# A gated long convolution with a squared-ReLU MLP: the short convolution's inputs laid out by time block and channel group

## The chip, the cores and the metric

The kernel runs on one core of a Trainium2 chip. The metric is device time in microseconds for one execution, median of several. The profile names the engines PE (TensorE, matmuls), PEld (its weight loads), DVE (VectorE), ACT (ScalarE), POOL (GpSimd) and SP (SyncE, which here only issues DMA transfers). SBUF is the on-chip memory with 128 partitions, PSUM the accumulator memory that matmuls write, here used as 8 banks of 512 floats per partition.

## What is computed

Sequence length S = 2048, D = 640 channels, F = 1728, everything float32.

```python
mod = (silu(c) @ w_mod).reshape(6, D)              # sa, ca, ga, sb, cb, gb
h = layernorm(x) * (1 + ca) + sa                   # x = A_q
k_shift[t] = sum(k[t - j] * shift_k[:, j] for j in range(4))
kv = k_shift * v
y = causal_conv(kv, ssm_k) + kv * ssm_D            # per channel, length 2048, by FFT of length 4096
x = x + ga * (h * y)
h = layernorm(x) * (1 + cb) + sb
x = x + gb * (relu(h @ w1 + b1) ** 2 @ w2 + b2)
```

## The kernel before

**Two stages.** The first computes the gated convolution, channel block by channel block (5 blocks b of 128 channels). The second is the MLP, over 8 chunks n of 256 rows and 14 slices f of F. The MLP's matmuls take operands split in a high and a low part (`hring`, `xt`, `w_S...`, `w_W`).

**The convolution as matmuls.** Time is split as t = 64 n + i (n is its upper part, 0 to 31, i its lower part, 0 to 63). Two operands per block have n and a channel sub-index a (0 to 3) on the 128 partitions and (32 channel groups, 64 values of i) along the free dimension: tile `p`, whose half 0 is kv and whose half 1 is ssm_k. `unit_a` transforms over n with the small table in `cst` (128 calls for each operand of a block, 256 instructions: the profile's `ps<-cst,p` of 64x64), ACT copies the result into tiles `a`; `spectra` transforms over i with the table `gb` (`ps<-a,gb`); for block 0 the filter's spectra are made first and kept (`early_h`, tiles `hs`); `front` multiplies the two spectra on DVE and combines on POOL (tiles `wx`); `back` and `unit_y` transform back with the tables `gi` (`ps<-gi,wx`) and `ca`; `prep` and `finish` apply layernorm, gate and residual and store the new x to DRAM (`x_d`). Each fp32 matmul call becomes two matmul instructions in the trace, a transpose one.

**Where kv comes from.** `kv_load` brings k and v in their natural layout, time on partitions, in pieces of 512 times by 128 channels (256 KB, runs of 512 bytes). `kv` turns each piece with four PE transposes (`ps<-ident,KV`) so that channels lie on partitions and time along the free dimension. ACT writes the first tap's product (scale by a per-partition `tap`), DVE adds the three others with SCALAR_TENSOR_TENSOR, each reading the transposed piece shifted by one more column; the three columns at a piece's end go through `ktail` and, from block 1 on, through small POOL products `kover`. Then v is transposed, DVE multiplies (`KV<-ps,KV`), and the product goes to a DRAM buffer `kv_d` [640 channels, 2048 times]. `load_x` reads it back in the layout of tile `p` (runs of 256 bytes). `load_h` brings ssm_k in the same layout (20 pieces, 128 partitions each); `skip` adds ssm_D to its value at time 0 on POOL.

**Tables.** `gb` and `gi` are loaded whole (2 MB each, 4 pieces each).

**Modulation rows.** `mod_sum(j)` loads five pieces of w_mod (`wm`), scales each on ACT by silu(c), and adds them on POOL; `mod_row` sums over partitions with two matmul calls against a tile of ones (`ps<-wm,ones`). The last gate row is made instead by `w_gate` matmuls whose weights are silu(c) broadcast to 128 columns.

**Order.** The program is a graph of steps; `order` places the steps of each engine in a list by priorities from a table `URGE`, and each engine then runs its list in order. Buffers have named slots that are handed on in order (`KACC`, `KN`, `UT` are parts of tile `KV`; `work` parts of `WX`). PSUM: any of 8 banks (`ANY`). SP's transfers are issued in order, and each waits until the fourth one before it has landed (`OUT = 4`, in `sp_issue`, L591):

```python
    def sp_issue(o, i):
        nc.sync.dma_start(o, i)
        queued.append(nc.cur_bb.bb.instructions[-1].name)
        if len(queued) > OUT:
            info = mybir.DependencyInfo(mybir.DependencyClass.Sync, mybir.DependencyReason.DATA)
            tc.add_manual_dep(nc.cur_bb.bb.instructions[-1], queued[-1 - OUT], info, reason="place in time")
```

Nearly all other instructions are issued from one place and carry L402 in the profile, so they are told apart by their tiles.

## Time and profile before

| | us |
|---|---|
| median of 3 runs | 699.93 (695.98 to 700.84) |
| the profiled execution's own time | 702.44 |
| its span, first to last instruction | 700.7 |
| mean granted TensorE clock | 0.978 |
| PE busy in the span | 648.1 |
| DVE, ACT, POOL busy | 389.4, 326.4, 253.8 |
| bytes moved by DMA | 74.45 MB |

Times below are those of the profiled execution, counted from the start of its span; its own time is 1.7 us above its span and 2.5 us above the median. The MLP's first matmul of chunk 0 comes at about 299 us, so the span is 299 us of the first stage and 402 us of the second.

### The profile page before, as it was taken

The page shows a single profiled execution, that of the slowest core. Times are in us where ns is not written, and L with a number is a line of the kernel's source. Part 1 is how long each engine was busy: PE and PEld are TensorE (multiplying, and loading weights), DVE is VectorE, ACT ScalarE, POOL GpSimd, SP SyncE. Part 2 cuts the span into 40 slices and gives each one's busy share as a digit, 9 for nine tenths or more (in the row PEclk, how much of TensorE's full clock was granted, in tenths as well). Part 3 has the DMA queues.
Part 4 walks back from the last instruction along what each step waited for, and adds up shares of the span by engine and source line. Part 5 has one row for each costly group of instructions (what it writes and reads, how often), then busy time and mean ns, then how long its engine had stood idle before and what let it go on. Part 6 is the DMA issues. An engine that isn't in the chain of part 4 may idle for free.

```text
span 700.7 us, 17805 instructions
## 1 busy us (share of the span) xinstructions
PE 648.1 (92%) x7513; PEld 582.6 (83%) x7513; DVE 389.4 (56%) x780; ACT 326.4 (47%) x678; POOL 253.8 (36%) x316
## 2 busy tenths in 40 slices
PE   3867998879988999899999999999999999999996
PEld 3766876758877787599999889999999999999996
DVE  0726866576769555875262464375354463563532
ACT  3643667776867786554332253224233243242220
POOL 1125765676867659643211321004013021030000
PEclk9999999998999999999999999999999999999999
DMA  9989889899885535542020020020020020110011
GB/s 245 244 243 294 251 238 225 211 253 220 194 196 135 145 78 182 157 135 61 1 76 1 0 76 1 1 76 1 1 75 1 5 73 2 36 40 1 0 39 38
DMA packets 108788, 74.45 MB, mean 106 GB/s; under 512 B 48546, under 2 KB 95650, under 8 KB 108708
## 3 DMA queue, kind: packets, MB, share of 16 engines
q1 hardware_dynamic: 101600, 70.24, 37.1%
q10 hardware_dynamic: 7044, 3.07, 2.4%
q8 instruction: 59, 0.97, 0.6%
q14 instruction: 21, 0.17, 0.1%
q0 software_dynamic: 64, 0.01, 0.0%
HBM read 58.88 MB, written 14.42 MB: 105 GB/s over the span
## 4 chain that ended last, share of the span: by engine, by line
PE 84%; DMA 6%; issue 3%; DVE 3%; ACT 2%; POOL 1%; SPq 0%; DVEq 0%; ACTq 0%; POOLq 0%
PE ps L402 84%; DMA p<-in_A_ssm_k_dram 2%; DMA KV<-in_A_k_dram 2%; DMA KV<-in_A_v_dram 1%; DVE KV L402 1%; DMA gb<-in_gb_dram 1%; DMA kv_d<-kacc 1%; ACT a L402 1%; DVE up L402 1%; DVE xt L402 0%; ACT KV L402 0%; POOL xt L402 0%; DVE wx L402 0%; SPq L591 0%; POOL x L402 0%
## 5 line engine op out<-in xcount | busy, mean ns | idle before, releaser
L402 PE MATMUL ps<-xt,w_S 128*128 128x512 f32 (+1 forms) x935 | 177.4, 331 | 3.6 <-POOL xt L402 1.6
L402 PEld LDWEIGHTS ps<-xt,w_S 128*128 128x128 f32 x935 | 142.8, 190 | 18.2 <-POOL xt L402 2.1
L402 PE MATMUL ps<-w_S,hring 128*128 128x320 f32 x648 | 109.0, 310 | 0.0
L402 ACT ACTIVATE mtmp<-ps,b1t 128x256 f32<-128x256 f32 (+1 forms) x112 | 51.5, 473 | 115.8 <-PE ps L402 111.4
L402 PEld LDWEIGHTS ps<-w_S,hring 128*128 128x128 f32 x648 | 99.2, 188 | 2.1
L402 PEld LDWEIGHTS ps<-a,gb 128*64 128x64 f32 x1280 | 74.6, 144 | 14.7 <-issue 5.9
L402 PE MATMUL ps<-a,gb 128*64 128x128 f32 x1280 | 83.5, 286 | 3.2 <-DVE wx L402 2.0
L402 DVE TENSOR_TENSOR mtmp<-ps,mtmp 128x256 f32<-128x256 f32 (+1 forms) x99 | 41.2, 420 | 81.4 <-ACT mtmp L402 80.5
L402 PE MATMUL ps<-cst,p 64*64 64x64 f32 x2560 | 50.0, 229 | 23.3 <-issue 12.2
L402 PEld LDWEIGHTS ps<-cst,p 64*64 64x64 f32 x2560 | 44.6, 142 | 31.1 <-issue 14.2
L402 DVE TENSOR_TENSOR hring<-mtmp,hring 128x256 fp32r<-128x256 f32 x74 | 37.3, 510 | 53.3 <-ACT hring L402 52.8
L402 POOL TENSOR_TENSOR wx<-wx 128x256 f32<-128x256 f32 x80 | 58.5, 750 | 16.5 <-DVE wx L402 12.2
L402 POOL TENSOR_TENSOR x<-x,gb2row 128x640 f32<-128x640 f32 x16 | 25.3, 1593 | 93.3 <-ACT mtmp L402 92.5
L402 ACT ACTIVATE hring<-mtmp 128x256 fp32r<-128x256 f32 x74 | 30.2, 414 | 60.6 <-PE ps L402 48.7
L402 ACT ACTIVATE a<-ps 128x512 f32<-128x512 f32 x80 | 45.5, 625 | 23.8 <-PE ps L402 23.6
L402 PE MATMUL ps<-w_S,w_W 128*128 128x320 f32 x312 | 52.7, 308 | 0.0
L402 DVE TENSOR_TENSOR wx<-ps,wx 128x512 f32<-128x512 f32 x64 | 41.1, 680 | 17.3 <-PE ps L402 15.0
L402 POOL TENSOR_TENSOR x<-mtmp,x 128x640 f32<-128x640 f32 (+1 forms) x9 | 13.0, 1450 | 100.4 <-DVE mtmp L402 100.4
L402 PEld LDWEIGHTS ps<-w_S,w_W 128*128 128x128 f32 x312 | 48.1, 188 | 1.1
L402 POOL TENSOR_TENSOR mtmp<-mtmp 128x256 f32<-128x256 f32 (+1 forms) x21 | 14.5, 690 | 83.8 <-ACT mtmp L402 83.5
L402 PE MATMUL ps<-gi,wx 64*128 64x128 f32 x640 | 41.0, 279 | 3.1 <-issue 2.3
L402 POOL TENSOR_TENSOR xt<-xfs,xt 128x256 fp32r<-128x256 f32 x35 | 28.3, 816 | 42.6 <-ACT xt L402 42.5
(130 smaller groups left out, 1070.1 us busy)
## 6 DMA issues: line engine op xcount, KB each, us to landing
wm<-in_w_mod_dram SPq DMA_DIRECT2D x25, 320.0 KB, 3.9
p<-in_A_ssm_k_dram SPq DMA_DIRECT2D x20, 256.0 KB, 5.9
KV<-in_A_k_dram SPq DMA_DIRECT2D x20, 256.0 KB, 4.4
KV<-in_A_v_dram SPq DMA_DIRECT2D x20, 256.0 KB, 4.5
p<-kv_d SPq DMA_DIRECT2D x20, 256.0 KB, 4.5
q<-in_A_q_dram SPq DMA_DIRECT2D x7, 640.0 KB, 7.2
out_dram<-x SPq DMA_DIRECT2D x14, 320.0 KB, 3.6
w1s<-in_B_w_dram SPq DMA_DIRECT2D x13, 320.0 KB, 3.5
```

Of the source, the lines that this page charges most:

```text
L402: fn(*real, **{k: a.real() if isinstance(a, View) else a for k, a in kw.items()})
```

## The change

The short convolution is made directly in the layout of tile `p`. The 640 channels are split in three groups s of 128, 256 and 256 channels (`BASE`, `WIDE`); a group's partition is 32 a + n, its free dimension is (i, channel within a). k and v come in 10 units u of 1024 elements per partition (two of group 0, four each of groups 1 and 2), each as four DMAs of 32 partitions (131 KB, runs of 128 bytes in group 0 and of 256 bytes in the others). A unit of k carries three more columns in front, the times before its own, copied on ACT from the unit before or, in the first, loaded by eight small DMAs that ACT issues. The taps are columns broadcast over i, so a tap's product is a tensor-tensor multiply. The first product goes to a two-bank PSUM tile, the others to SBUF; in groups 0 and 1 two of the four products are on POOL (`KP`); DVE adds them up in PSUM and multiplies by v into the operand of `unit_a`, tile `px` (names `S0p`, `S1p` in the order). There are no transposes of k and v, and no `kv_d`. ssm_k comes in four DMAs of 32 partitions per block.

Also changed: half of `gb` and of `gi` is loaded, the other half is made by ACT with sign changes (a few columns come from `cst`); the modulation rows j = 0, 1, 2 are made as the last gate row was, by ten matmul calls each with weights silu(c) broadcast (`sg4`, which lies in `XP0p`, and `sg1`), without ACT and POOL; q for the gating comes in pieces by channel group s, 128 or 256 channels wide; steps other than these units may use six PSUM banks; `ssm_D` is loaded straight into place by eight small POOL transfers; `URGE` is a new table.

```diff
-        "gb": gb.reshape(128, 4096).astype(f),
-        "gi": gt.reshape(128, 64, 2, 2, 16).transpose(0, 1, 3, 4, 2).reshape(128, 4096).astype(f),
+        "gb": gb[:, :, 0].reshape(128, 2048).astype(f),
+        "gi": gt[:, :, 0].reshape(128, 2048).astype(f),
...
-    banks = [one(i) for i in range(8)]
+    banks = [one(i) for i in range(8)] + [(("B6", "B7"), lambda s, d, n: shaped(last[: s[0]], s))]
...
-    ANY = (0, 1, 2, 3, 4, 5, 6, 7)
+    ANY = (0, 1, 2, 3, 4, 5)
+    BOTH = (8,)
...
+    BASE, WIDE, MATES = (0, P, 3 * P), (DG, 2 * DG, 2 * DG), ((0,), (1, 2), (3, 4))
+    SB = (0, 1, 1, 2, 2)
...
     def mod_sum(j):
+        ts = [psum(f"mr_{j}_{i}", (P, 320), MR) for i in range(2)]
+        for b in range(NB):
+            t = stg(f"wm_{j}_{b}")
+            sp_dma(t, w_mod[b * P : (b + 1) * P, j * D : (j + 1) * D], 2560)
+            for i in range(2):
+                with g.as_one(0.53):
+                    mm(ts[i], sgb(b), t[:, 320 * i : 320 * i + 320], b == 0, b == NB - 1)
...
     def load_gb(i):
+        sp_dma(gb[:, 0, o], gb_d.rearrange("p (g a f) -> p g a f", g=16, a=2)[:, o], 4096)
+        act.activation(gb[0:64, 1, o], gb[64:128, 0, o], AF.Copy, scale=-1.0)
+        act.activation(gb[64:128, 1, o], gb[0:64, 0, o], AF.Copy)
     def load_gi(i):
+        sp_dma(gi[:, 0, o], gi_d.rearrange("p (g c n) -> p g c n", g=16, c=2)[:, o], 4096)
+        act.activation(gi[:, 1, o, 0], gi[:, 0, o, 1], AF.Copy, scale=-1.0)
+        act.activation(gi[:, 1, o, 1], gi[:, 0, o, 0], AF.Copy)
...
-    def kv_load(b, h):
-    def kv(b, h, kn):
...
-            for j in range(4):
-                turn(tk[:, j * P : (j + 1) * P], kn[:, 0, j], hold=[acc])
-        act.activation(acc[:, c:], tk[:, c:], AF.Copy, scale=tap[:, b, 0:1])
-        for t in (1, 2, 3):
-            dve.scalar_tensor_tensor(o, tk[:, : 512 - t], tap[:, b, t : t + 1], o, op0=ALU.mult, op1=ALU.add)
-        dve.tensor_mul(acc, tv, acc)
-        sp_dma(in_dram(kv_d, to, b * P, b * P + P, 1 << h), acc, 2048)
...
+    def load_kv(s, u):
+        w = WIDE[s]
+        n = 1024 // w
+        kt = KT[s, u] = sbuf(f"k_{s}_{u}", (P, n + 3, w), KS, line="K")
+        if u == 0:
+            pool.memset(kt[:, 0:3], 0.0)
+        else:
+            copy(act, kt[:, 0:3], KT[s, u - 1][:, n : n + 3])
+        for a in (0, 2, 1, 3):
+            cols = slice(BASE[s] + w * a, BASE[s] + w * a + w)
+            if u == 0:
+                act_dma(kt[32 * a + 1 : 32 * a + 17, 0:3], kshift[0:16, 0:3, cols], 4 * w)
+                act_dma(kt[32 * a + 17 : 32 * a + 32, 0:3], kshift[16:31, 0:3, cols], 4 * w)
+            sp_dma(kt[32 * a : 32 * a + 32, 3:], ksrc[:, n * u : n * u + n, cols], 4 * w)
+        vt = VT[s, u] = sbuf(f"v_{s}_{u}", (P, n, w), VS, line="V")
+        for a in (0, 2, 1, 3):
+            sp_dma(vt[32 * a : 32 * a + 32], vsrc[:, n * u : n * u + n, cols], 4 * w)
+
+    def kv(s, u):
+        acc = psum(f"kacc_{s}_{u}", (P, n, w), BOTH)
+        for t in range(4):
+            o = sbuf(f"ktmp_{s}_{u}_{t}", (P, n, w), TMP) if t else acc
+            own = t > 1 and s in KP
+            mul(pool if own else dve, o, kt[:, 3 - t : 3 - t + n], taps[:, t].unsqueeze(1).to_broadcast([P, n, w]), hold=[] if own else [acc])
+            if t:
+                add(dve, acc, acc, o)
+        for b in MATES[s]:
+            c = slice(beta(b), beta(b) + DG)
+            mul(dve, px[b][:, :, n * u : n * u + n].rearrange("p g i -> p i g"), acc[:, :, c], vt[:, :, c])
...
+    def load_h(b):
+        for a in (0, 2, 1, 3):
+            c = BASE[SB[b]] + WIDE[SB[b]] * a + beta(b)
+            sp_dma(t[32 * a : 32 * a + 32], hsrc[:, c : c + DG], 256)
+        pool.tensor_add(t[:, :, 0], t[:, :, 0], dsm[:, b])
...
     URGE = {
-        ("b1", 0): [-1812, -1830],
+        ("b1", 0): [-1209, -1601],
```

In the order below, each row is one instruction or several alike (xN), written as output<-inputs and shape; a number at the end of a name is the buffer's. On SP, before: SP's list around the store and the re-load of block 0's kv (`kacc0` is block 0's product, `p_0` its operand tile, `gi` the table).

```order
L591 DMA p_1_146<-in_A_ssm_k_dram 128x8x64
L591 DMA kv_d_98<-kacc0_231 128x512 x4
L591 DMA KV_87<-in_A_k_dram 128x4x128 x2
L591 DMA gi_379<-in_gi_dram 128x1024
L591 DMA KV_87<-in_A_v_dram 128x4x128
L591 DMA kv_d_98<-KV_87 128x512
L591 DMA p_0_102<-kv_d_98 128x8x64 x2
```

And now, from the tenth row of SP's list, the end of group 0's k and v (32x32x32), the first two of ssm_k's four pieces for block 0 (`S1p`), and group 1's first pieces (32x16x64):

```order
L617 DMA KV_87<-in_A_k_dram 32x32x32
L617 DMA gb_134<-in_gb_dram 128x1024
L617 DMA KV_87<-in_A_v_dram 32x32x32 x3
L617 DMA gi_144<-in_gi_dram 128x1024
L617 DMA KV_87<-in_A_v_dram 32x32x32
L617 DMA S1p_150<-in_A_ssm_k_dram 32x32x64 x2
L617 DMA KV_87<-in_A_k_dram 32x16x64 x4
L617 DMA KV_87<-in_A_v_dram 32x16x64
```

The store and the re-load are gone, and ssm_k's pieces, which were first in the queue, stand behind all of group 0's k and v.

On PE, before: the end of the first transform of ssm_k (`p_102`) and the first transposes of k (`ident,KV`), rows 47 to 53 of its list.

```order
L402 MATMUL ps_90<-cst,p_102 64x64 x2
L402 MATMUL ps_91<-cst,p_102 64x64 x2
L402 MATMUL ps_97<-ident,KV 128x128 x4
L402 MATMUL ps_96<-ident,KV 128x128 x4
L402 MATMUL ps_95<-ident,KV 128x128 x4
L402 MATMUL ps_94<-ident,KV 128x128 x4
L402 MATMUL ps_93<-ident,KV 128x128 x4
```

And now, rows 142 to 151, between the spectra of block 0 (`a_0`): the modulation row's matmuls (`wm` pieces by the broadcast silu(c) in `XP0p`).

```order
L402 MATMUL ps_93<-a_0_342,gb 64x128 x8
L402 MATMUL ps_94<-wm_0_553,XP0p 128x320
L402 MATMUL ps_94<-wm_1_565,XP0p 128x320
L402 MATMUL ps_95<-wm_0_553,XP0p 128x320
L402 MATMUL ps_94<-wm_2_589,XP0p 128x320
L402 MATMUL ps_90<-a_0_186,gb 64x128 x8
L402 MATMUL ps_94<-wm_3_603,XP0p 128x320
L402 MATMUL ps_95<-wm_1_565,XP0p 128x320
L402 MATMUL ps_95<-wm_2_589,XP0p 128x320
L402 MATMUL ps_95<-wm_3_603,XP0p 128x320
```

PE's list now starts with the first transform of block 0's kv (`S0p`, 128 calls) and goes on with that of ssm_k (`S1p`); the 160 transposes of k and v are gone, and 24 more modulation calls stand in the early part.

## The prediction on record

> **What bounds the kernel now.** I read the table of stretches first, cut where it matters for this change: 0 to 34, 0 to 89 and 89 to 299 us, one disturbed stretch, and the MLP. Columns: stretch, length, busy us of PE, PEld, DVE, ACT, POOL, granted clock, DMA share, GB/s.
>
> ```profile
> 0.00:34.00 34.00, 20.66 (x400) 18.27 (x402) 13.26 (x30) 15.82 (x29) 4.81 (x17) 1.00 0.94 244
> 0.00:89.00 89.00, 62.51 (x1517) 55.50 (x1520) 46.38 (x91) 43.10 (x80) 31.71 (x62) 0.96 0.90 257
> 89.00:299.00 210.00, 191.57 (x3457) 155.64 (x3445) 146.26 (x237) 150.41 (x296) 144.71 (x175) 0.96 0.74 185
> 120.00:160.00 40.00, 31.53 (x586) 24.99 (x584) 25.54 (x40) 31.16 (x65) 26.09 (x28) 0.89 0.91 232
> 299.00:701.00 402.00, 393.99 (x2556) 371.44 (x2556) 196.78 (x453) 132.88 (x303) 77.34 (x79) 0.99 0.11 32
> ```
>
> In the MLP PE is busy 394 of 402 us; nothing the change touches works there, so I keep that stretch. In the first 299 us PE works 254.1 us and idles 44.9: 26.5 before 89 us, beside DMA engines that are 90% busy, and 18.4 after. The second view is who PE waits for, first until 89 us, then until 299 (us in total, times, longest).
>
> ```profile
> PE ps L402 <- DMA gb<-in_gb_dram: 9.1, 1, 9.1
> PE ps L402 <- DMA KV<-in_A_k_dram: 7.4, 4, 4.9
> PE ps L402 <- issue: 7.3, 5, 2.4
> ...
> PE ps L402 <- issue: 8.8, 6, 2.3
> PE ps L402 <- DVE KV L402: 3.4, 3, 2.7
> PE ps L402 <- DVE wx L402: 2.0, 1, 2.0
> ```
>
> Early, PE waits for the first data (until 9.1 us) and for k; later for its own instructions ("issue"), and for the short convolution on DVE. So the stage is PE's work plus a start set by DMA, and the change must be priced in three sums: PE's work, when data arrive, and DVE.
>
> **PE's work.** The groups by shape (columns: count, busy us, mean ns):
>
> ```profile
> L402 PE MATMUL ps<-ident,KV 128*128 128x128 f32 x160 | 27.7, 314 | 12.3 <-DMA KV<-in_A_k_dram 7.4 <-DVE KV L402 2.7 <-issue 1.6
> L402 PE MATMUL ps<-cst,p 64*64 64x64 f32 x2560 | 50.0, 229 | 23.3 <-issue 12.2 <-DMA gb<-in_gb_dram 9.1 <-POOL p L402 1.4
> L402 PE MATMUL ps<-wm,ones 128*128 128x320 f32 x12 | 5.2, 532 | 0.0
> L402 PE MATMUL ps<-w_gate 128*128 128x320 f32 x20 | 6.7, 448 | 0.0
> ```
>
> Removed: 160 transposes, 27.7 us, and the six modulation calls (12 instructions), 5.2. Added: 30 calls in the form of the gate's ten, 6.7/10 = 0.67 each, 20.1. Net 27.7 + 5.2 - 20.1 = 12.8 us less work, all of it inside the first 299 us. Everything else on PE keeps its count.
>
> **When data arrive.** The transfers (KB each, median us from issue to landing):
>
> ```profile
> p<-in_A_ssm_k_dram SPq DMA_DIRECT2D x20, 256.0 KB, 5.9
> KV<-in_A_k_dram SPq DMA_DIRECT2D x20, 256.0 KB, 4.4
> p<-kv_d SPq DMA_DIRECT2D x20, 256.0 KB, 4.5
> kv_d<-KV SPq DMA_DIRECT2D x16, 256.0 KB, 3.9
> gb<-in_gb_dram SPq DMA_DIRECT2D x4, 512.0 KB, 4.9
> w2s<-in_B_w_dram SPq DMA_DIRECT2D x2, 160.0 KB, 2.8
> ```
>
> Removed: store and re-load of kv, 20 pieces of 256 KB each way, 10.5 MB, and half of both tables, 2.1 MB. At the 257 GB/s of the first stretch these 12.6 MB are 49 us of transfer time. Against that, k, v and ssm_k (15.7 MB) now come in pieces of 32 partitions, which no row shows. With four in flight, the 160 KB pieces (2.8 us, 64 partitions) would give 4 x 160/2.8 = 229 GB/s, the 256 KB pieces of ssm_k, in runs of 256 bytes as the new ones, 4 x 256/5.9 = 174. I take 190, nearer to the row with the same runs; then the 15.7 MB need 83 us where 257 GB/s would need 61. Net some 27 us less for the DMA engines, in a stage whose later part isn't bound by them.
>
> [...]
>
> The start, by SP's new order. The first PE call needs all of group 0's k and v: 2.1 MB at 190 = 11 us, and before their last piece the taps and the first pieces of both tables, 1.4 MB at 257 = 5.4; with 0.7 us to the first issue, 2 for the last landing and one DVE product (below) PE starts at about 21 us, where it started at 9.1:
>
> ```profile
> 9.13 1.99 PE L402 MATMUL ps<-cst,p 64*64 64x64 f32 x64 [9.13 <-DMA gb<-in_gb_dram]
> ```
>
> It then has 256 instructions at 50.0/2560 = 0.0195, 5 us, and waits for ssm_k of block 0, whose fourth piece has 2.1 MB of 32-partition pieces and 0.5 MB of table ahead of it: 11 + 2 us more, 34 with the POOL addition. Everything on PE is queued behind these two waits, and on ACT the first copies of `a`. So PE idles 29 us in the first 34; before it idled 34 - 20.7 = 13.3.
>
> I then compare equal progress: both lists reach a place where 64 `back` calls and 144 calls of spectra are done, before at 89 us, now at row 300. Up to there the new list has 256 first-transform instructions less (5.0 us), no transposes (76 of them, 76 x 0.173 = 13.1), and 20 modulation calls instead of 2 (+11.7): 62.5 - 5.0 - 13.1 + 11.7 = 56.1 us of work, 51 of it after 34 us. That gives 85, and 87 with one stall of the "issue" kind. Row 300 needs block 1's kv: of group 1 and what SP has between, 4.2 MB at 190 and 6.4 MB at 257, 22 + 25 us after 33, 80 us, and the last unit's sums. So the place is reached at 87 instead of 89: the late start is paid back by transposes that are gone and by waits for k that are gone. I put -2.
>
> From there to the MLP the work is 254.1 - 12.8 - 56.1 = 185.2 us. Of the 18.4 us of idle time the 8.8 of "issue" stay, since the first transform that starves PE of instructions is as long as before; the 3.4 on the convolution and some of the rest, which come in a knot of ACT, DVE and POOL at 120 to 160 us, go with the work taken from ACT. I take 12. 185.2 + 12 = 197, against 210: -13.
>
> **DVE, ACT and POOL.** The rows for the price:
>
> ```profile
> L402 DVE SCALAR_TENSOR_TENSOR KV<-ps,tap,KV 128x511 f32<-128x511 f32 x16 | 12.0, 749 | 3.7 <-ACT ktail L402 1.8 <-ACT KV L402 1.5
> L402 DVE TENSOR_TENSOR KV<-ps,KV 128x512 f32<-128x512 f32 x20 | 13.7, 686 | 7.4 <-PE ps L402 4.4 <-ACT wx L402 1.9
> L402 DVE TENSOR_TENSOR mtmp<-ps,gbrow 128x320 f32<-128x320 f32 x32 | 14.3, 484 | 12.0 <-PE ps L402 11.6
> L402 DVE TENSOR_TENSOR up<-up,row 128x512 f32<-128x512 f32 x8 | 5.5, 691 | 8.2 <-ACT up L402 8.2
> L402 DVE TENSOR_TENSOR up<-up,KV 128x512 f32<-128x512 f32 x8 | 8.3, 1064 | 1.5 <-POOL KV L402 1.5
> L402 DVE TENSOR_TENSOR wx<-ps,hs 128x512 f32<-128x512 f32 x16 | 10.1, 683 | 3.9 <-PE ps L402 3.9
> L402 DVE BATCH_NORM_STATS2 s<-q 128x6 f32<-128x320 f32 x30 | 13.1, 473 | 0.0
> L402 POOL TENSOR_TENSOR KV<-KV,row 128x512 f32<-128x512 f32 x12 | 16.7, 1402 | 5.0 <-DVE KV L402 3.5 <-DVE row L402 1.4
> L402 POOL TENSOR_TENSOR wm<-wm,wm 128x640 f32<-128x640 f32 x20 | 31.0, 1550 | 16.6 <-ACT wm L402 11.1 <-ACT ktail L402 5.4
> L402 POOL TENSOR_SCALAR kover<-ktail,tap,kover 128x1 f32<-128x1 f32 x36 | 14.3, 407 | 1.6
> L402 ACT ACTIVATE wm<-wm,sg 128x640 f32<-128x640 f32 x25 | 20.4, 824 | 1.0 <-DMA wm<-in_w_mod_dram 0.8 <-issue 0.2
> L402 ACT ACTIVATE KV<-ps,tap 128x512 f32<-128x512 f32 x4 | 2.8, 688 | 3.8 <-PE ps L402 3.8
> ```
>
> DVE loses 20 x (3 x 0.749 + 0.686) = 58.7 us. An operation with a PSUM operand costs 0.484 at 320 and 0.686 at 512 columns, so 1.22 at 1024. DVE gains 30 sums, 10 products into PSUM and 2 last products at 1.22 (51.2), 16 half-wide last products at 0.686 (11.0), and 18 products from SBUF to SBUF, which no row shows at this size: twice 0.691 to twice 1.064, 25 to 38 us; I take 27, since POOL helps in only twelve products. Sum 89, 30 more than before, and DVE's load in the stage goes from 192.6 to about 223 of 285 us. That is hidden as long as no unit's product is what PE waits for.
>
> POOL gains 12 products of 2 x 1.402 (34) and loses 12 of the 20 `wm` additions (18.6) and `kover` (14.3): even. ACT loses 20 first products (13.8) and 15 scalings (12.4) and gains eight table halves, four of 512 columns (0.69 each) and four of 1024 (up to twice that), 7, and seven short copies and some 31 more DMA issues; these take ACT's queue 0.36 to 0.64 us each:
>
> ```profile
> 1.28 0.64 ACTq L514 DMA_DIRECT2D cst<-in_cw_dram  x1
> 4.30 0.36 ACTq L521 DMA_DIRECT2D cst<-in_ca_dram  x1
> ```
>
> 11 to 20 us, so ACT is even too. The two banks reserved for the units leave six for the rest; among PE's longest waits above none is for ACT, which frees most banks, so I charge nothing, and 3 us at the upper end.
>
> **The sum.** 702.4 (profiled execution) - 2 - 13 = 687.4; that execution is 2.5 above the median, so against the median it is 684.9. I forecast 686, between the two, and 676 to 697 for this case: the DMA bounds (229 and 174 GB/s instead of 190) are worth -4 and +2 us at the start, those of the idle time after 89 us (6 and 18 for 12) -6 and +6, the PSUM banks +3.
>
> **The rivals.** *DVE comes late (slower).* A product that reads two SBUF tiles took 691 ns in one group and 1064 in another of the same shape, the latter next to POOL's additions on the same tiles. [...] On the traced numbers: up to the last product of block 1, DVE's list holds 18 sums, 12 flat products, the last products, 16 spectra products (0.683) and 15 statistics (0.473), 66 us at the low price and 75 at the high one, from about 9 us on. If DVE is busy 85% of the time there, block 1 is ready at 9 + 75/0.85 = 97 instead of 87, and group 2's 16 flat products on DVE repeat it: +10 and +12, 708. It decides when DVE's idle time up to there exceeds 12 us at the low price, 3 at the high one. For it: DVE was idle 43 of the first 89 us, waiting for data, and much of that may stay. Against: at half load a late unit has room to catch up. *The pieces are slow (slower).* If a 131 KB piece takes nearly as long as a 256 KB one, the rate with four in flight falls to 125 GB/s (at 5.9 us it would be 89). Then the start, ssm_k and group 1 each lose 6, 6 and 12 us: +12 to +23, 698 to 709. Against: the 160 KB rows at 2.8 us. *PE's idle time stays.* The work goes, but PE's idle time after 89 us stays at 18.4 since "issue" and PSUM take its place: -6, and nothing at the start: 694 to 699. *More comes back.* With 229 GB/s the early place is reached 5 us sooner, idle after 89 us falls to 5 (-7 more), and the clock, 0.89 in the disturbed stretch (3.5 us of its 31.5), comes back: 686 - 5 - 7 - 4 = 670, down to 667. That the change does not do what it says is excluded by the order: no transposes, no `kv_d`.
>
> **Chances.** Forecast 0.45, more 0.16, idle stays 0.10, DVE late 0.17, slow pieces 0.12. A change of 1%, 7 us, is about what a measurement of this kernel can tell from none. Under 693: 0.40 of the forecast, all of "more", 0.01 of the third: 0.57. Over 707: most of DVE late (0.13) and of the slow pieces (0.09): 0.22. Between: 0.21. Range 667 to 711: it leaves out the worse halves of the two slow cases.
>
> **What would show it.** PE's first matmul at 19 to 23 us, the second wait (for ssm_k, POOL's addition) ending at 31 to 37. The first 131 KB pieces landing in 2.5 to 3.2 us; over 4 speaks for the slow pieces. Groups: sums at 1.2 us, flat products at 1.4 to 1.6 on DVE, 2.8 on POOL; near 2.1 on DVE, with PE waiting for `S0p` or `S1p` after 80 us, speaks for DVE. The MLP's first matmul near 284 us, the rest of the span again 402; PE busy about 635. I am wrong if PE's idle time before 299 us is not near 43, or if the MLP's 402 us move.

## The result: slower, 737.5 us, and the profile after

| | before | after |
|---|---|---|
| median of 4 runs each, us | 700.38 (695.98 to 703.63) | 737.49 (735.78 to 739.45) |
| ratio, 95% interval | | 1.0535 (1.047 to 1.06) |
| span of the profiled execution, us | 700.70 | 737.70 |

I cut both profiled executions at two places of equal progress. The first is the prediction's: block 0's 64 `back` calls and 144 calls of spectra are done, and PE goes on (before at 89.18 us with block 0's `unit_y`, after at 113.37 with the first transform of block 1's kv, which before had done by then). The second is the MLP's first matmul (295.69 and 329.55; the prediction's round 299 was a little late). The table of stretches, first of before, then of after; columns: stretch, length, busy us of PE, PEld, DVE, ACT, POOL, granted clock, DMA share, GB/s.

```profile
0.00:89.18 89.18, 62.69 (x1520) 55.61 (x1520) 46.38 (x91) 43.10 (x80) 31.71 (x62) 0.96 0.90 257
89.18:295.69 206.51, 189.28 (x3432) 153.91 (x3427) 142.95 (x235) 150.37 (x295) 141.84 (x174) 0.96 0.74 184
295.69:700.70 405.01, 396.10 (x2567) 373.06 (x2567) 200.09 (x455) 132.92 (x303) 80.21 (x81) 0.99 0.12 33
```

```profile
0.00:113.37 113.37, 56.87 (x1224) 47.92 (x1225) 81.14 (x80) 43.70 (x60) 61.71 (x53) 0.95 0.82 167
113.37:329.55 216.18, 191.16 (x3610) 152.54 (x3611) 169.69 (x226) 160.88 (x278) 127.71 (x126) 0.95 0.58 140
329.55:737.70 408.15, 398.30 (x2567) 374.17 (x2567) 202.02 (x450) 132.85 (x303) 79.27 (x81) 0.99 0.11 32
```

The 37.0 us between the two spans are +24.2 at the start, +9.7 in the middle, +3.1 in the MLP. PE's idle time (length less its busy time) goes from 26.5 to 56.5 at the start, from 17.2 to 25.0 in the middle, from 8.9 to 9.9 in the MLP. PE's work at the start fell as forecast (62.7 to 56.9); the start is lost by waiting alone.

Who PE waits for after, until 340 us (us in total, times, longest):

```profile
PE ps L402 <- DMA KV<-in_A_k_dram: 43.2, 1, 43.2
PE ps L402 <- ACT a L402: 12.7, 18, 2.1
PE ps L402 <- DVE wx L402: 8.5, 6, 3.3
...
PE ps L402 <- issue: 2.2, 3, 0.9
```

One wait of 43.2 us stands first. The name on it, a transfer of k, is only the end of what the chain was followed back to; the timelines show what lay between. After's DVE, one POOL row and PE, each row with its start, length and, in brackets, the idle time before it and who ended that:

```profile
16.65 1.97 DVE L402 TENSOR_TENSOR up<-KV 128x1024 f32<-128x1024 f32 x1 [4.82 <-DMA KV<-in_A_k_dram]
18.54 4.64 DVE L402 TENSOR_TENSOR ps<-KV 128x1024 f32<-128x1024 f32 x1
...
30.27 1.23 DVE L402 TENSOR_TENSOR ps<-ps,up 128x1024 f32<-128x1024 f32 x1 [4.49 <-POOL up L402]
...
41.25 1.95 DVE L402 TENSOR_TENSOR S0p<-ps,KV 128x1024 f32<-128x1024 f32 x1
```

```profile
16.67 4.67 POOL L402 TENSOR_TENSOR up<-KV 128x1024 f32<-128x1024 f32 x1 [3.94 <-DMA KV<-in_A_k_dram]
```

```profile
43.25 4.82 PE L402 MATMUL ps<-cst,S0p 64*64 64x64 f32 x192 [43.25 <-DMA KV<-in_A_k_dram]
50.19 1.65 PE L402 MATMUL ps<-cst,S0p 64*64 64x64 f32 x64 [2.12 <-ACT a L402]
52.91 0.48 PE L402 MATMUL ps<-cst,S1p 64*64 64x64 f32 x4 [1.08 <-POOL S1p L402]
```

From 16.65 to 43.2 the first two units run through DVE and POOL: 26.6 us of products and sums, one after another (in 4.5 of them DVE waits for POOL), before PE has anything to do. And while PE waits, the queue behind it stands still. After's SP queue, and the transfers (KB each, median us from issue to landing):

```profile
24.03 5.71 SPq L617 DMA_DIRECT2D S1p<-in_A_ssm_k_dram  x2
35.47 1.90 SPq L617 DMA_DIRECT2D KV<-in_A_k_dram  x4
```

```profile
KV<-in_A_k_dram SPq DMA_DIRECT2D x40, 128.0 KB, 3.7
S1p<-in_A_ssm_k_dram SPq DMA_DIRECT2D x20, 256.0 KB, 5.3
```

Group 1's k goes out from 35.5 us; POOL ends its last product of group 0 at 33.0 and only then clears the extra columns of the next k tile. And the first 20 us, first of before, then of after:

```profile
0.00:20.00 20.00, 8.45 (x200) 7.64 (x201) 0.91 (x4) 6.73 (x11) 3.21 (x13) 1.00 0.95 241
```

```profile
0.00:20.00 20.00, 0.00 (x0) 0.00 (x0) 3.61 (x5) 3.26 (x5) 9.46 (x19) 1.00 0.91 121
```

121 GB/s with the DMA engines 91% busy, where before moved 241 at 95%.

The groups of after that answer to the priced ones (columns: count, busy us, mean ns, idle time before them), and under them the one of before that the prediction did not look at. `up<-KV` and `ps<-KV` are the products of k with a tap into SBUF and into PSUM (the former are the prediction's "flat" ones), `S0p<-ps,KV` the last products, with v:

```profile
L402 PE MATMUL ps<-cst,S1p 64*64 64x64 f32 x1536 | 32.7, 241 | 12.5 <-ACT a L402 5.4 <-POOL S1p L402 4.2 <-DVE wx L402 1.7
L402 PE MATMUL ps<-cst,S0p 64*64 64x64 f32 x1024 | 24.6, 255 | 50.3 <-DMA KV<-in_A_k_dram 43.2 <-ACT a L402 3.9 <-DVE S0p L402 2.1
L402 PE MATMUL ps<-wm,XP0p 128*128 128x320 f32 x48 | 15.1, 448 | 0.3 <-DMA wm<-in_w_mod_dram 0.2
L402 ACT ACTIVATE a<-ps 128x512 f32<-128x512 f32 x80 | 77.3, 1105 | 20.0 <-PE ps L402 19.7
L402 DVE TENSOR_TENSOR ps<-KV 128x1024 f32<-128x1024 f32 x10 | 27.3, 2728 | 0.1
L402 DVE TENSOR_TENSOR ps<-ps,up 128x1024 f32<-128x1024 f32 x30 | 36.9, 1231 | 7.2 <-POOL up L402 6.1
L402 DVE TENSOR_TENSOR S0p<-ps,KV 128x512 f32<-128x512 f32 x12 | 12.2, 1057 | 2.2 <-DMA KV<-in_A_v_dram 2.1
L402 POOL TENSOR_TENSOR up<-KV 128x1024 f32<-128x1024 f32 x12 | 38.0, 3188 | 27.7 <-DVE ps L402 16.6 <-DMA KV<-in_A_k_dram 11.0
```

```profile
L402 ACT ACTIVATE a<-ps 128x512 f32<-128x512 f32 x80 | 45.5, 625 | 23.8 <-PE ps L402 23.6
```

Eighty copies of `a` have the same shape before and after, and cost 625 and 1105 ns. Their line differs in one letter's place: `a` now holds its columns as (e d g) instead of (g e d), so that the copy, which still runs over d innermost, writes 128 bytes apart.

### The profile page after: what moved, and what is told of

It reads as the page before. It is cut to its first block, busy times and chain, and to the rows that moved or that the text cites. A ratio compares the mean times of both kernels' runs of the same rounds, so it can differ in the third digit from the quotient of the medians.

```text
span 737.7 us, 17486 instructions
## 1 busy us (share of the span) xinstructions
PE 646.3 (88%) x7401; PEld 574.6 (78%) x7401; DVE 452.9 (61%) x754; ACT 337.4 (46%) x639; POOL 268.7 (36%) x259
## 4 chain that ended last, share of the span: by engine, by line
PE 74%; DVE 7%; DMA 7%; ACT 6%; issue 3%; POOL 3%; SPq 0%; ACTq 0%; DVEq 0%; POOLq 0%
PE ps L402 74%; ACT a L402 5%; DMA KV<-in_A_k_dram 2%; DVE up L402 2%; DMA KV<-in_A_v_dram 2%; DVE ps L402 1%; POOL up L402 1%; DVE wx L402 1%; DMA wm<-in_w_mod_dram 1%; DVE mtmp L402 1%; DMA gb<-in_gb_dram 1%; DMA S1p<-in_A_ssm_k_dram 1%; POOL wx L402 0%; SPq L617 0%; ACTq L402 0%
## 5 line engine op out<-in xcount | busy, mean ns | idle before, releaser
L402 PE MATMUL ps<-xt,w_S 128*128 128x256 f32 (+1 forms) x680 | 129.3, 331 | 0.0
L402 PEld LDWEIGHTS ps<-xt,w_S 128*128 128x128 f32 x680 | 104.8, 190 | 10.3 <-DVE xfs L402 0.2
L402 ACT ACTIVATE a<-ps 128x512 f32<-128x512 f32 x80 | 77.3, 1105 | 20.0 <-PE ps L402 19.7
L402 PE MATMUL ps<-w_S,hring 128*128 128x320 f32 x456 | 78.0, 310 | 0.0
L402 PEld LDWEIGHTS ps<-w_S,hring 128*128 128x128 f32 x456 | 70.1, 188 | 1.4
L402 PE MATMUL ps<-cst,S0p 64*64 64x64 f32 x1024 | 24.6, 255 | 50.3 <-DMA KV<-in_A_k_dram 43.2
L402 POOL TENSOR_TENSOR up<-KV 128x1024 f32<-128x1024 f32 x12 | 38.0, 3188 | 27.7 <-DVE ps L402 16.6
L402 DVE TENSOR_TENSOR up<-KV 128x1024 f32<-128x1024 f32 x18 | 43.0, 2396 | 5.3 <-DMA KV<-in_A_k_dram 4.8
L402 DVE SCALAR_TENSOR_TENSOR mtmp<-mtmp 128x256 f32<-128x256 f32 x91 | 44.9, 500 | 1.8
L402 ACT ACTIVATE wx<-ps 128x512 f32<-128x512 f32 x49 | 29.5, 608 | 32.3 <-PE ps L402 29.1
```

Of the source, the lines that this page charges most:

```text
L402: fn(*real, **{k: a.real() if isinstance(a, View) else a for k, a in kw.items()})
```

## The experiments

All edits are to the changed kernel. "Place" is where the first stretch above ends (before 89.2, after 113.4 us), "middle" the length of the second (206.5 and 216.2); ratios are to the kernel before, with 95% intervals. Places and stretches are from one profiled execution each.

**The copies of `a` and the taps.** The first edit lets the copy run over g innermost:

```
-            copy(act, o, t[e].rearrange("p g m d -> p m g d"))
+            copy(act, o.rearrange("p m g d -> p m d g"), t[e].rearrange("p g m d -> p m d g"))
```

> One line changed: the ACT copies of the first transform into tiles a run with the channel index g innermost, so eight floats in a row are written at consecutive addresses and read from PSUM 256 bytes apart (in the changed kernel two floats are read side by side and written 128 bytes apart). The order of every engine stays. Theory A (the strided write is what makes the 80 copies take 1105 ns instead of 625, and PE's 12.7 us of waits for a come from that): copies at 600 to 750 ns, PE's waits for a under 5 us, 722 to 730 us. Rival B (what costs is any access that isn't pairs on both sides, or the copies hide beside other work): copies at 1000 ns or more, or shorter copies and a time of 734 to 740.

The second reads each tap's channels side by side instead of 16 bytes apart:

```
-        taps = tapb[:, at : at + 4 * w].rearrange("p (c t) -> p t c", t=4)
+        taps = tapb[:, at : at + 4 * w].rearrange("p (t c) -> p t c", t=4)
```

> The taps are read as consecutive floats (the tile is taken as tap by channel, where the changed kernel takes channel by tap, 16 bytes apart); it is loaded as before, so the products use other taps. The order of every engine stays. Theory A (the 16-byte stride makes DVE's product of 1024 elements take 1.96 us undisturbed instead of the 1.4 that I forecast): undisturbed products at 1.3 to 1.5 us on DVE and fewer than 2.8 on POOL, 2 to 6 us less time, 731 to 736. Rival B (two SBUF operands set the rate, whatever their stride): 1.9 to 2.0 us again, 736 to 739. Both expect DVE's products to take over 4 us where a POOL product runs beside them.

Copies: 734.6 us, 1.0466 (1.0428 to 1.0504). Taps: 731.1 us, 1.0426 (1.0386 to 1.0465). The copies' group with the first edit:

```profile
L402 ACT ACTIVATE a<-ps 128x512 f32<-128x512 f32 x80 | 43.1, 599 | 30.7 <-PE ps L402 26.0 <-DMA KV<-in_A_k_dram 4.5
```

and the flat products on DVE, first of after, then with the second edit (ns: least, median, most):

```profile
L402 DVE TENSOR_TENSOR up<-KV x18: 1962/2106/3393, 16.6 to 219.1; 128x1024 f32<-128x1024 f32 x18
```

```profile
L402 DVE TENSOR_TENSOR up<-KV x18: 1208/1245/3395, 16.8 to 212.2; 128x1024 f32<-128x1024 f32 x18
```

So the price of both operations is the layout: 1105 to 599 ns by the loop's order alone, 2106 to 1245 by the spacing of one operand. Yet the middle falls by 2 us only in each (214.0 and 214.2). Did each hide the other? Both edits together:

> The changed kernel's own order throughout, with two edits: the copies into a with the channel index innermost, and the taps read as consecutive floats (other taps, as in the run that did this alone). Alone they gained 3 and 6 us. Theory A (ACT's copies and DVE's products hide each other in the stretch from the equal-progress place to the MLP, 218 us long): both together gain 14 to 20 us, most of it in that stretch, which falls to 203 to 209; 718 to 724 us. Rival B (the gains add): 727 to 730, the stretch at 211 to 214.

725.2 us, 1.0323 (1.0285 to 1.0361). The stretches of that run:

```profile
0.00:110.14 110.14, 55.56 (x1225) 46.52 (x1225) 71.99 (x80) 34.36 (x60) 53.31 (x53) 0.95 0.87 171
110.14:316.10 205.96, 185.42 (x3610) 148.73 (x3611) 156.08 (x226) 139.86 (x278) 127.17 (x126) 0.98 0.61 148
```

Yes. The middle is 206.0, as long as before's, 10.2 less than after's. PE's idle time there falls from 25.0 to 20.5, and the same 3610 instructions take 185.4 instead of 191.2 us, at a granted clock of 0.98 instead of 0.95. Every later version with cheap copies and with taps cheaper or left out has a middle of 204 to 209 us, and no version with one of these two edits alone is under 214.

**Pieces or the unit chain.** Two causes for PE's late start were open: the slow transfers, and the chain of products. Runs of 4096 bytes for k and v in pieces of the same size (from other places of k and v, so the values are others; the line for v alike):

```
-            sp_dma(kt[32 * a : 32 * a + 32, 3:], ksrc[:, n * u : n * u + n, cols], 4 * w)
+            sp_dma(kt[32 * a : 32 * a + 32, 3:], klong[:, u, a], 4 * w)
```

> Each 131 KB piece of k and v is read from one place of k or v as runs of 4096 bytes instead of 128 or 256: the same bytes, pieces, partitions and order, but other elements of k and v, so the values of kv are others. Theory A (the short runs set the late start): the pieces land in 2.5 us or less instead of 3.7 and 4.5, PE's first matmul comes at 30 to 35 instead of 43.2 us (the two units' chain of DVE and POOL work stays, some 26 us behind the first product), and the time falls by 8 to 14, to 724 to 730. Rival B (the chain of products and sums sets the start, not the transfers): PE's first matmul at 39 or later and 733 to 739. Rival C (start earlier, but the gain is lost again at a later wait): first matmul at 35 or earlier, time within 4 us of 737.5.

Group 0's units with one tap of the four:

```
+            if n.key in (("kv", 0),) and n.nth % (9 if n.key[1] else 8) in range(1, 7):
+                continue
```

> Left out: in the two units of group 0 the products of taps 1 to 3 and their sums (six products, two of each unit on POOL, and six sums on DVE); kv of these 128 channels has one tap. All transfers and the order of what is left stay. Theory A (PE's empty start is bounded by the chain of products and sums, and is paid one for one at the end): PE's first matmul at 27 to 33 instead of 43.2 us, time 723 to 728 us. Rival B (transfers bound the start as soon as the chain is shorter): first matmul at 36 or later, 731 to 738. Rival C (the start is earlier but ssm_k of block 0, next in PE's list and behind group 0 in SP's, takes the wait over): first matmul at 33 or earlier, S1p's first use still at 48 or later, 731 to 736.

Runs: 735.1 us, 1.0479 (1.0436 to 1.0523), place 110.3. One tap: 734.8 us, 1.0435 (1.0389 to 1.0481), place 111.3. With one tap PE starts at 30.9 instead of 43.2, but ssm_k's first use moves from 52.9 to 50.1 only, for PE now waits for ACT (us in total, times, longest; after had 2.1 as the longest):

```profile
PE ps L404 <- ACT a L404: 23.2, 18, 12.1
```

The long runs' first 20 us, and SP's queue in that run:

```profile
0.00:20.00 20.00, 0.00 (x0) 0.00 (x0) 4.83 (x5) 3.15 (x5) 10.67 (x19) 1.00 0.59 147
```

```profile
21.16 12.84 SPq L617 DMA_DIRECT2D S1p<-in_A_ssm_k_dram  x2
34.22 3.07 SPq L617 DMA_DIRECT2D KV<-in_A_k_dram  x4
```

The engines are busy 59% at 147 GB/s instead of 91% at 121, so these short runs do cost engine time; what keeps 147 below before's 241 stays open. But SP comes to ssm_k 2.9 us earlier only to take longer from there to group 1's k, 13.1 us instead of 11.4, which goes out at 34.2 instead of 35.5. With one tap it goes out at 30.3: its buffers are held by the chain. Each cause hides the other again. Both edits at once, and then eight transfers in flight instead of four, alone (`queued[-1 - 8]`) and on top:

> Two earlier runs in one: pieces of k and v read as runs of 4096 bytes (other values), and taps 1 to 3 of group 0 left out. Each alone gained 2 to 3 us. Theory A (two limits of nearly equal length stand at the start, the transfers and the chain of products and sums that frees the buffers for SP's next pieces, so that removing one leaves the other): S1p's first use at 34 to 42 instead of 52.9, the equal-progress place at 95 to 104 instead of 113.4, time 720 to 729. Rival B (what holds the equal-progress place lies behind the start, in group 1's units or in the modulation rows' transfers): the place at 107 or later, 731 or more, as with either alone.

> SP waits for the eighth transfer before the one it issues, not the fourth; every list of instructions stays in its order. Four pieces of 131 KB that take some 4.1 us each are 128 GB/s, and the first 20 us moved 121. Theory A (the limit of four pieces in flight, which are half as large as before, holds the early stream back): over 170 GB/s in the first 20 us, k's pieces landing in under 5 us, PE's first matmul at 36 to 40, S1p's first use before 49 us, 4 to 9 us less: 728 to 734. Rival B (the DMA engines, 91% busy in those 20 us, are full with runs of 128 bytes): 120 to 135 GB/s again, k's pieces landing in 6 us or more, 735 to 741.

> The run with long runs and one tap in group 0, and in addition eight transfers in flight. Theory A: three limits of the same stream, each of which hides the next: S1p's first use at 30 to 36, the place at 88 to 100, 714 to 725 us. Rival B: nothing beyond the run with two edits, within 3 us of it.

Both: 728.2 us, 1.0339 (1.0286 to 1.0391), place 102.2: 11.2 us earlier, where the two alone gave 3.1 and 2.1; group 1's k goes out at 26.6. Eight in flight: 739.6, 1.0513 (1.0458 to 1.0567), as after; on top of both, 730.7, 1.0387 (1.0318 to 1.0455), no gain. The first 20 us with eight alone:

```profile
0.00:20.00 20.00, 0.00 (x0) 0.00 (x0) 3.37 (x5) 3.26 (x5) 9.23 (x19) 1.00 0.89 118
```

With these short runs more in flight does not raise the rate, and the engines are as busy as before that edit; with long runs and one tap, eight in flight moved 159 instead of 148. With both limits gone a third shows, on ACT, in the run with both edits (start, length, idle before):

```profile
38.70 2.12 ACT L404 ACTIVATE gb<-gb 64x1024 f32<-64x1024 f32 x2 [5.52 <-DMA gb<-in_gb_dram]
40.85 7.25 ACT L404 ACTIVATE a<-ps 128x512 f32<-128x512 f32 x8
```

The second table half's transfer and copies stand ahead of the copies of `a`, and PE waits for those.

**The rest of the products, and everything at once.** One tap in all three groups; then that with long runs, eight in flight and the cheap copies:

> Left out: in all ten units the products of taps 1 to 3 and their sums (18 products and 30 sums on DVE, some 80 us, and 12 products on POOL, 38 us). All transfers and the order of what is left stay. Theory A (the late start is most of the loss, the rest of the short convolution's arithmetic is largely hidden): as the run that leaves them out in group 0 alone, and 2 to 8 us more: 716 to 724 us. Rival B (DVE's and POOL's arithmetic for the short convolution is the whole loss, through its waits after the start): 698 to 708 us. Rival C (transfers): 730 or more.

> All suspects out at once: long runs of k and v (other values), taps 1 to 3 left out in all groups, eight transfers in flight, and the copies into a with the channel index innermost. Theory A (stream, chain, DVE's and POOL's arithmetic and the copies are the whole loss): the place at 85 to 97, the MLP's first matmul at 285 to 300, 692 to 706 us. Rival B (something not yet named, in the lists' order or in PE's own work, holds the rest): 712 or more.

725.4 us, 1.0321 (1.0279 to 1.0362), place 108.7, and 714.2 us, 1.013 (1.0077 to 1.0183). The former's middle is 207.8 with the dear copies of `a`: products left out altogether do there what cheaper taps alone don't. In the latter the middle is 206.1, the MLP 406.3, and the place 102.0: of the 13.8 us by which the span of its profiled execution is still longer than before's, 12.9 lie in the start.

**The filter first.** The other way to an early PE is ssm_k ahead of k and v, as before. Asked of the planner by two due times, and then by moving only SP's first pieces and what uses them, all other rows kept as in the changed kernel:

```
-        ("lgb", 0): [-137, -306],
+        ("lgb", 0): [5, -306],
...
-        ("lh", 0): [-285, -215, -205, -371, -416],
+        ("lh", 0): [9, 8, 7, 6, 9],
```

> Order only: ssm_k of block 0 and the first half of gb are put ahead of k and v of group 0 in SP's list, so that PE begins with the filter's transform and its first eight spectra steps (block 0's h stage) and does them while k and v come; nothing else is taken out or added. Theory A (of the 37 us that the changed kernel is slower, a large part is PE's 43 us of empty start, because its first item waits for all of group 0): PE's first matmul at 9 to 13 us, first use of S0p at 47 to 54, the equal-progress place 10 to 16 us earlier, 723 to 729 us. Rival B (kv's later units and ACT's copies set the pace after the start): PE starts early but waits longer for S0p or S1p of block 1, and the time stays at 733 to 740.

> Order only, and only at the start: SP brings the four pieces of k of the first unit, then ssm_k of block 0 and half of gb, then the rest of group 0; PE does the filter's first transform and its eight spectra steps ahead of the first use of S0p, ACT the copies that belong to them. Every other step stands in the changed kernel's own order on its engine (the run with the filter first before this one had let the planner place everything anew). Theory A (PE's empty start costs what it shows): PE's first matmul at 11 to 17, first use of S0p at 40 to 48, the equal-progress place 12 to 18 us earlier than 113.4, time 719 to 726 us. Rival B (after the start DVE's units or ACT's copies set the pace and the gain is waited away): the equal-progress place less than 6 us earlier, 732 to 738 us.

769.1 us, 1.098 (1.0953 to 1.1007): the planner placed everything anew, so this says little of the move itself. Kept in place: 746.1 us, 1.0607 (1.0565 to 1.0649). PE, in the latter:

```profile
17.42 7.14 PE L406 MATMUL ps<-cst,S1p 64*64 64x64 f32 x256 [17.42 <-POOL S1p L406]
...
72.12 4.72 PE L406 MATMUL ps<-wm,XP0p 128*128 128x320 f32 x8 [11.63 <-DMA wm<-in_w_mod_dram]
```

PE starts at 17.4 instead of 43.2, and reaches the place at 115.9 instead of 113.4. Its idle time up to there falls only from 56.5 to 49.9, with the longest wait now for the modulation weights, and the same work takes 66.0 us instead of 56.9, at a granted clock of 0.85 instead of 0.95. Then with the cheap copies and with taps laid side by side by two ACT copies for each group (nothing left out); with long runs, one tap in all groups and the cheap copies, both table halves first and the modulation pieces earlier on SP; and this order again with nothing left out:

> Three edits together: the start's order with the filter first, the copies into a with the channel index innermost, and the taps made consecutive by six small ACT copies through PSUM (the taps are the right ones). If the gains add, 737.5 less 16, 3 and 6: 710 to 715 us. If the order takes over what the taps gained at the start (4 of their 6 us): 714 to 719. Against the kernel before, at 700, both are slower by about 2%. If it is 705 or less, the parts hid behind each other and the changed layout costs nothing but these three.

> The run with all suspects out, with four transfers in flight as in the changed kernel, and with the start's order turned: k of the first unit, ssm_k of block 0 and both halves of gb first, the filter's transform and spectra ahead of S0p on PE, and the first modulation row's pieces of w_mod spread before and between group 1's pieces. Left out as there: taps 1 to 3 of all groups; k and v in long runs have other values. Theory A (with everything in time, the place is where PE's 57 us of work end after its real start; the loss at the start was the lists' order for a stream that is slower than they assume): PE's first matmul at 12 to 17, no wait over 5 us after it until the place, the place at 78 to 92, 692 to 706 us. Rival B (group 1's kv or w_mod are the limit whatever the order): the place at 98 or later, 710 or more.

> The run with three edits (correct taps made consecutive, copies with the channel index innermost, filter first), with both halves of gb ahead of v, POOL's four products of group 0 in the order of the units, and the first modulation row's pieces of w_mod earlier in SP's list. That run's PE waited 9.9 us for the table's second half, 13.4 for w_mod, and DVE 8.9 for POOL. Theory A (those waits held the place at 114): the place at 96 to 106, 709 to 719 us. Rival B (one stream of transfers, moving w_mod forward pushes group 1 back): the place at 110 to 118, 724 to 731.

727.6 us, 1.0352 (1.031 to 1.0394), place 114.2; 719.1 us, 1.0243 (1.0196 to 1.0291), place 105.3; 730.9 us, 1.041 (1.036 to 1.0461), place 116.4. PE's longest wait after the start, in the second and the third of these:

```profile
70.60 1.97 PE L408 MATMUL ps<-a,gb 128*64 128x128 f32 x16 [17.57 <-DVE wx L408]
```

```profile
79.71 1.97 PE L406 MATMUL ps<-a,gb 128*64 128x128 f32 x16 [22.61 <-DVE wx L406]
```

Now PE waits for a spectra product (`wx`) that stands on DVE behind group 1's units, and these wait for their transfers; DVE in the second of the three:

```profile
59.55 1.89 DVE L408 TENSOR_TENSOR S0p<-ps,KV 128x512 f32<-128x512 f32 x2 [18.07 <-DMA KV<-in_A_v_dram]
62.52 1.97 DVE L408 TENSOR_TENSOR ps<-KV 128x1024 f32<-128x1024 f32 x1 [1.08 <-issue]
64.40 1.88 DVE L408 TENSOR_TENSOR wx<-ps,XP0p 128x512 f32<-128x512 f32 x3
```

In no order was the place earlier than 102 us.

**ssm_k between the groups.** On the kernel with long runs and one tap, then with nothing left out (side-by-side taps, cheap copies): the second table half and block 0's ssm_k ahead of group 1's k and v on SP, and POOL's and ACT's rows to match.

> The run with long runs of k and v (other values) and one tap in group 0, and in addition three steps moved ahead of group 1's: SP brings the second half of gb and ssm_k of block 0 before any piece of group 1, POOL adds ssm_D before group 1's products, and ACT copies group 1's extra columns after the first copies into a. PE's and DVE's orders stay. In that run PE began at 27.4 us, waited 10.2 us for ACT (held by the second table half), and used S1p first at 45.6; in all runs in this order the equal-progress place came 57 to 61 us after S1p's first use. Theory A (the late place is the late start of block 0's two operands, plus PE's own 57 us): S1p's first use at 33 to 39, the place at 90 to 98, 716 to 724 us. Rival B (group 1, now later in the queue, takes over): S1p at 33 to 39, but the place at 101 or later and 726 or more.

> Nothing left out, nothing wrong in value: the changed kernel with consecutive taps (six small ACT copies), the copies into a with the channel index innermost, and the same three steps moved ahead of group 1's. The run with the first two edits alone was at 725. Theory A: S1p's first use at 43 to 48 instead of 51, the place at 101 to 107, 715 to 721 us. Rival B (group 1 is pushed back as much): the place at 108 to 114, 722 to 728. Neither expects it to reach the kernel before, at 700.

734.5 us, 1.0476 (1.0403 to 1.0549), and 727.6 us, 1.0385 (1.0323 to 1.0447). In the first ssm_k is used at 37.3 instead of 45.6 us, and the place is 109.8 instead of 102.2; on the way PE stands here:

```profile
54.55 0.69 PE L408 MATMUL ps<-a,gb 128*64 128x128 f32 x4 [12.67 <-ACT a L408]
```

The copies of `a` that PE waits for stand on ACT behind the copy of group 1's extra columns, which waits for group 1's k:

```profile
53.11 0.36 ACT L408 ACTIVATE KV<-KV 128x192 f32<-128x192 f32 x1 [12.55 <-DMA KV<-in_A_k_dram]
53.38 5.67 ACT L408 ACTIVATE a<-ps 128x512 f32<-128x512 f32 x6
```

The best two that leave nothing out and change no values are at 727.6 us; no version beats the kernel before.

## Why the prediction was wrong

The forecast was 687.4 for the profiled execution, and it was 739.45: 52 us, of which the start has 26 (+24.2 for -2), the middle 23 (+9.7 for -13), the MLP 3. Two steps failed. The first is the start, "the late start is paid back by transposes that are gone": PE began at 43.25 us for 21, and block 1's kv, for which the sum had 80 us and the last unit's sums, was there at 113. The second is the middle's -13, which rested on "ACT is even", on flat products of 1.5 us and on 12 us of idle time. Either was enough to turn the sign: with the other as forecast, the kernel would still be 11 to 14 us slower. PE's idle time before the MLP, 43 us by the prediction's own test, was 81.5.

- *PE's work.* The counts held: no transposes; the 60 modulation instructions took 19.4 us (the 48 above 15.1, the 12 with `sg1` 4.3), where 20.1 was forecast; the start's 56.9 us stands for 56.1. But 12.8 us less before the MLP became 3.9 (251.97 to 248.03): the first transform's 2560 instructions took 57.3 us instead of 50.0. Cut at the MLP's first matmul, the forecast's middle work is 183.1 us (251.97 - 12.8 - 56.1; the prediction's 185.2 reaches to 299 us); measured were 191.2, and 185.4 with the cheap copies and taps, for the same 3610 instructions. The granted clock was 0.95 and 0.98 in these two. That isn't the whole of it, since before had 0.96; why the first transform took 7.3 us more stays open.
- *When PE starts.* "One DVE product" after the last piece was the largest omission. A unit is a chain of products and sums over DVE and POOL; two units came to 26.6 us, so PE began at 43.25 and not at 21, and used ssm_k at 52.9 and not at 34. With one tap PE began at 30.9, with long runs at 42.1. The rate was the second: 190 GB/s taken, 121 measured, which the rival of slow pieces had (125). Before's rows had the direction (pieces of 256 KB took 4.4 us in runs of 512 bytes, 5.9 in runs of 256), and the measured 121 is below both rates that 190 was taken from (229 and 174). Either limit alone is nearly enough for this part of the delay: removing one gave 2 to 3 us of the place, removing both 11.2.
- *From ssm_k's first use to the place.* Forecast 87 - 34 = 53 us, measured 113.4 - 52.9 = 60.5. With 18.9 us from the first use itself that is the 26.4 by which the place was late. Of the 24.2 us lost against before, 11.2 are the two limits above. For the other 13, each new order moved the wait, to the modulation weights, to ACT's copies, to DVE behind group 1, but the place stayed, and the traces show what it stands behind. As the prediction said ("Row 300 needs block 1's kv"), it needs group 1's last unit. After's DVE and PE there:

```profile
112.29 1.92 DVE L402 TENSOR_TENSOR S0p<-ps,KV 128x512 f32<-128x512 f32 x2 [2.06 <-DMA KV<-in_A_v_dram]
```

```profile
113.37 0.69 PE L402 MATMUL ps<-cst,S0p 64*64 64x64 f32 x32 [1.92 <-DVE S0p L402]
```

In all versions but the one planned anew, the place comes 1.1 to 2.6 us after this row of DVE begins, and the row begins 72 to 81 us after group 1's first k goes out (after: 35.5 and 112.3). The prediction's sum had 22 + 25 = 47 us for that stream, and 10.6 MB; after moved 14.4 MB in it, 188 GB/s over 76.8 us. So an earlier PE is waited away, and the two limits above count by how early they let group 1's k go out (26.6 instead of 35.5). That this stream alone sets the place is read from the traces and not shown by a run: none shortened it. Nor did a run untie block 0 from group 1 in the in-order lists of SP, ACT and DVE.

- *DVE, ACT and POOL.* The sums were right (1.23 for 1.22 us). The flat products were not (1.5 us taken; 1.96 at the least, 2.11 the median), nor the products into PSUM (2.73 for 1.22), nor the half-wide last products (1.06 for 0.686). Before the MLP DVE got 61.5 us more instead of 30. "ACT is even" was wrong in a step I had not made: nothing about the copies of `a` seemed changed, and they cost 31.8 us more; in all, ACT had 11.1 us more to do before the MLP. Together these two, copies and flat products, are the middle's 10 us, as the run with both edits shows. What the runs changed is the spacing: 16 bytes between taps made 1245 ns into 2106 (medians), 128 bytes between the copies' writes 599 into 1105 (means); why it costs that is not shown.
- *Idle time in the middle.* 12 forecast, 25.0 found, 20.5 with both edits. So even with right prices the forecast's -13 there does not come; before's 206.5 is what does. The "issue" waits that I kept (8.8 us) fell to 2.2 there and were 6.2 again with the cheap copies, 7.3 with both; that PE waited for others first fits this.
- *The rivals.* "The pieces are slow" (698 to 709) had the rate right, and "DVE comes late" (708) the price of a flat product, though most of that price is the spacing of the taps (2.11 us, 1.25 side by side) and not POOL beside it. Both came at once, with the copies on top. The range, built from single cases, had no room for that.
- *The MLP* was kept and took 3.1 us more, 2.2 of it PE's work in the same 2567 instructions. The other versions have 405.6 to 408.3; the cause stays open.

## What to carry to other kernels

When a layout moves, price again every operation that reads or writes the moved tile, also those whose line and shape stay: ask what its innermost loop now steps over. A first matmul that hangs on element-wise work must be priced by the whole chain from the first landing, with the buffers that the chain holds and the queue that stands behind them. A place of equal progress must be priced by the last operand that it needs, in the queue's order, and not by PE's work alone. Where two limits are equally long, removing either shows almost nothing; remove both before calling one harmless.

## What the hardware showed that I had not expected

- A DVE product of two SBUF tiles took 4.64 us beside a POOL product that began 1.9 us before it, and ended 1.84 us after it, as if it had begun only then; without one it took about 1.97.
- Pieces of 32 partitions in 128-byte runs moved 121 GB/s in the first 20 us with four in flight and 118 with eight, with the DMA engines 91 and 89% busy.
- The ACT copies of 128x512 out of PSUM nearly doubled (599 to 1105 ns) by the order of their two innermost loops alone.
- The same 3610 matmul instructions cost PE 3% more at a granted clock of 0.95 than at 0.98. The run with the lower clock was also the one in which PE waited longer (25.0 and 20.5 us), but before had 0.96 with 17.2 us of waiting, so what sets the clock is not shown.
